# One transformer block on one core: the last 256 tokens as two tiles of 128, and denominators from sums of four key tiles

## The chip, the core and the metric

The kernel runs on one core of a Trainium2 chip. The metric is the device time of one execution in microseconds (us): the median of the runs. Beside the times there is a profile of one execution, taken by the hardware profiler. Engines are called PE (TensorE), ACT (ScalarE), DVE (VectorE), POOL (GpSimd) and SP (SyncE, which issues all DMAs here).

## The reference

x has 2048 tokens of 1024 features, bfloat16. H = 32 heads of 32 features, F = 3584.

```python
def _A_ref(x, wqkv, wo):
    qkv = (x @ wqkv).reshape(B, S, 3, H, Dh)  # then transposed: q, k, v by head
    scores = einsum("bhqd,bhkd->bhqk", q, k) * Dh ** -0.5
    p = softmax(scores, axis=-1)
    o = einsum("bhqk,bhkd->bhqd", p, v)
    return o.transpose(0, 2, 1, 3).reshape(B, S, D) @ wo

def _B_ref(x, w1, b1, w2, b2):
    h = gelu(einsum("bsd,df->bsf", x, w1) + b1, approximate=True)
    return einsum("bsf,fd->bsd", h, w2) + b2

h = x + _A_ref(layernorm(x), A_wqkv, A_wo)
h2 = h + _B_ref(layernorm(h), B_w1, B_b1, B_w2, B_b2)
```

## The kernel before

**Attention.** Four heads make a head group g (0 to 7), and 256 queries a block qb (0 to 7). A job is one (qb, g). It has 8 rounds of two key tiles of 128. `Att.qk` (L769) issues 8 matmuls of a round, four heads side by side in the rows of the array, into two units of two PSUM banks; ACT turns each unit of 1024 columns into P = exp(scale x score) in the ring PT (L779; 9 slots of one round). `Job.pv` (L805) multiplies P by V, four heads side by side in the columns, into one PSUM bank, whose columns 0 to 255 hold O and 256 to 511 the denominators. For these DVE adds the two key tiles of a round into a slot of PS (L820; 3 slots), and `Job.den` (L834) multiplies the sum by a block of ones, 4 matmuls; the last round of a job and the jobs of group 0 of blocks 0 and 1 go to `den` from PT directly, 8 matmuls. `finish` transposes, inverts and multiplies (L850 to L865) and writes OT, which has three slots, taken by u % 3.

**The rest.** Per block u of 256 tokens: `wo(u)` (output projection and residual), `ln2(u)` (LayerNorm, with its statistics on DVE, its powers on POOL, and transposes on PE, L604), `ffn1(u)` (14 blocks of w1, each 16 matmuls of 256 columns), GELU, and `ffn2(u, j)` for the two halves j of the output, each 28 matmuls of 512 columns for each of two token tiles. In blocks 0 to 6 DVE evicts FFN1 with the bias (L943), and GELU is built from five DVE operations and one Tanh on ACT (L962 to L967), for the exp's table holds Tanh too. The last block uses ACT's own GELU (L952) once exps are over (`tail=True`).

**Banks.** Units of scores take banks 0 to 5. Banks 6 and 7 are given out when needed (`Slot`): one bank to a job, for as long as it lasts, the other to the background work. With `tail=True` the banks 0 to 5 are used.

**Order.** No order is written by hand. `Graph.add` records each operation with the buffers that it reads and writes, and `schedule` plays a list scheduler over durations given in the code: `switch` for a change of PE's tiling mode, `c_dve`, `c_dve_ps`, `c_act` and fixed numbers. PE takes, by `pick_pe`, a QK as soon as one is ready, then PV and denominators by how many rounds wait, else background work in the order of the program; with nothing ready, a warming matmul (L1007) at the start. Each engine then executes its list in that order, with semaphore waits between engines. All durations change the order on each engine, but nothing else. Runs of column-tiled matmuls that are long enough are merged into full ones (`merge_tiles`: L537 is such a full matmul, L534 a column-tiled one, L540 one in the tail).

**The lead.** In the first 66 us the 16 rounds of group 0 of blocks 0 and 1 run between LayerNorm, transposes and first projections, on two units of PSUM. Then come the projections of the other groups in between the jobs.

**The end of the program text before:** `wo(6)`, `ffn2(5, ...)`, `ln2(6)`, `ffn1(6)` come after the attention of block 7 in the order of the program; then

```python
    ffn2(6, 0)
    wo(7, True)
    ln2(7, True)
    ffn2(6, 1, True, R1, (None, 5))
    ffn1(7, True)
    ffn2(7, 0, True, R1, (0, 1))
    ffn2(7, 1, True, R2, (2, 3))
```

where R1 are the weight rings that all blocks use, and R2 rings that lie over K and V, which are free by then.

Of the kernel before, what the change touches and what calls it, by code (L numbers as in the profile page):

```python
# [12 lines left out]
P = 128  # L13
# [47 lines left out]
class Graph:  # L61
# [47 lines left out]
    def schedule(self, pick_pe, pool, switch=0.1, dma_rate=280.0, dma_lat=2.1, dma_issue=0.06):  # L109
# [219 lines left out]
def build_kernel(nc, A_x, A_wqkv, A_wo, B_w1, B_b1, B_w2, B_b2, out):  # L329
# [22 lines left out]
    class Area:  # L352
        def __init__(self, start):
            self.cur = start
# [54 lines left out]
    B_OT = [B_OT_[G * i:G * i + G] for i in range(3)]  # L409
    xrb, B_xrb = sb(ot_lo, "xrb", [P, 8, D], BF, 8)  # L410
# [34 lines left out]
    gT7, B_gT7 = sb(Area(pt_lo), "gT7", [P, FC, 256], BF, FC // 2)  # L445
    gs, B_gs = [gT] * 7 + [gT7], [B_gT] * 7 + [B_gT7]
# [22 lines left out]
    att_area = Area(att_lo)  # L469
    w2_area = Area(att_lo)  # L470
    R2 = Rings((att_area, 14), (w2_area, 7), att_area, 2, "b_")
    assert att_area.cur <= att_hi
# [15 lines left out]
    def c_dve_ps(n):  # L488
        return (120 + n) / 960.0 + 0.02

    def c_dve(n, x=1):
        return (62 + n / x) / 960.0 + 0.085

    def c_act(n, ap_bias=False):
        return 0.073 + (0.093 if ap_bias else 0.0) + n / 1200.0

    def pe(fns, occ, reads=(), writes=(), kind="bg", mode="full", prio=0, after=()):
        return gr.add(E.PE, fns, occ, 0.16, reads, writes, prio, kind, mode, after)
# [45 lines left out]
    def act(fn, n, reads=(), writes=(), prio=0, ap_bias=False, kind="", after=()):  # L544
        return gr.add(E.Activation, fn, c_act(n, ap_bias), 0.14, reads, writes, prio, kind, after=after)

    def dve(fn, occ, reads=(), writes=(), prio=0):
        return gr.add(E.DVE, fn, occ, 0.08, reads, writes, prio)
# [25 lines left out]
    def layer_norm(tiles, prio, norm="dve", stats=None):  # L574
# [6 lines left out]
        for k, (x_ap, B_x, o_ap, B_o) in enumerate(tiles):  # L581
            for c in range(2):
                dve(lambda v, c=c, k=k, x_ap=x_ap: v.bn_stats(st_l[:, i + k, 6 * c:6 * c + 6], x_ap[:, 512 * c:512 * c + 512]),
                    0.68, reads=B_x if isinstance(B_x, list) else [B_x], writes=[B_stl[i + k]], prio=(prio or 1) if stats is None else stats)
# [11 lines left out]
        for k, (x_ap, B_x, o_ap, B_o) in enumerate(tiles):  # L596
            eng, cost = (dve, 0.58) if norm == "dve" else (pool, 3.8)
# [4 lines left out]
    def transposes(src_ap, B_src, bank, dst_ap, B_dst, evac, prio):  # L602
# [9 lines left out]
        else:  # L612
            t = dve(lambda v: v.tensor_copy(dst_ap, src()), 0.70, reads=[bb(bank)], writes=[B_dst])
# [133 lines left out]
    class Att:  # L747
# [8 lines left out]
        def qk(self, job, r):  # L756


            qb, g = job
            qs = q_slots[qb, g]  # L760
            us = [self.unit % self.n_units, (self.unit + 1) % self.n_units]
            self.unit += 2
            fns, banks = [], []
            for i in range(2):
                for h in range(4):
                    k0 = (2 * r + i) * P

                    def fn(p, i=i, h=h, k0=k0):
                        return p.matmul(psum[:, 2 * us[h // 2] + h % 2, 256 * i:256 * i + 256],  # L769
                                        KT[32 * h:32 * h + 32, g, k0:k0 + P], QT[32 * h:32 * h + 32, qs, :],  # L770
# [4 lines left out]
            pe(fns, 0.224, reads=[B_KT[8 * g + r], B_QT[qs]], writes=banks, kind="qk", mode="row")  # L775
# [11 lines left out]
    closing = set()  # L787

    class Job:


        def __init__(self, qb, g, bank):
            self.qb, self.g, self.bank = qb, g, bank
            self.B_O, self.B_D = (bank.buf, gr.buf()) if isinstance(bank, Slot) else (B_psO[bank], B_psD[bank])
            self.n = 0
            self.sums = []

        def pv(self, r, s):
            g, bank, first = self.g, self.bank, self.n == 0
            last = self.n == 7  # L800
            self.n += 1
            fns = []
            for i in range(2):
                for h in range(4):
                    fns.append(lambda p, i=i, h=h: p.matmul(  # L805
                        psum[32 * h:32 * h + 32, bi(bank), 0:256], V[:, g, 2 * r + i, 32 * h:32 * h + 32],
                        PT[:, s, h // 2, h % 2, 256 * i:256 * i + 256], start=first and i == 0, stop=last and i == 1,
                        tile_position=(0, 32 * h), skip_group_check=True))
            rd = [B_PT[2 * s], B_PT[2 * s + 1], B_V[NT * g + 2 * r], B_V[NT * g + 2 * r + 1]]
            t = pe(fns, 0.224, reads=rd, writes=[self.B_O, self.B_D] if first else [self.B_O], kind="pv", mode="col")  # L810
# [3 lines left out]
            if r == 7 or (self.g == 0 and self.qb < 2):  # L814
                self.sums.append((s, True))
            else:
# [5 lines left out]
                self.sums.append((n, False))  # L822
# [5 lines left out]
        def den(self, n, direct, last):  # L828
            bank = self.bank
            fns = []  # L830
            for i in range(2 if direct else 1):
                for h in range(4):
                    rhs = PT[:, n, h // 2, h % 2, 256 * i:256 * i + 256] if direct else PS[:, n, h, :]
                    fns.append(lambda p, h=h, rhs=rhs, i=i: p.matmul(  # L834
                        psum[32 * h:32 * h + 32, bi(bank), 256:512], ones32[:, :], rhs,
                        start=False, stop=last, tile_position=(0, 32 * h), skip_group_check=True))
            t = pe(fns, 0.224 if direct else 0.112, reads=[B_PT[2 * n], B_PT[2 * n + 1]] if direct else [B_PS[n]],
# [4 lines left out]
        def finish(self):  # L842
            qb, g, bank = self.qb, self.g, self.bank
            u = qb % 3
# [3 lines left out]
            final = qb == 2 * NCH - 1 and g == G - 1  # L848
            D = OD[:, o, 1, :].rearrange("p (b j) -> p b j", j=32)
            t = dve(lambda v: v.transpose(OD[:, o, 1, :], psum[:, bi(bank), 256:512]), 0.445,  # L850
                    reads=[self.B_O, self.B_D], writes=B_D, prio=-1)
            drop(t, bank)
            if final:
                t = act(lambda a: a.activation(OD[:, o, 0, :], psum[:, bi(bank), 0:256], ACT.Copy), 256,
                        reads=[self.B_O, self.B_D], writes=B_O, prio=-1, after=[t])
            else:
                t = dve(lambda v: v.tensor_copy(OD[:, o, 0, :], psum[:, bi(bank), 0:256]), c_dve_ps(256),  # L857
                        reads=[self.B_O, self.B_D], writes=B_O, prio=-1)
            drop(t, bank)
            dve(lambda v: v.reciprocal(rr[:, o, :], D[:, :, 0]), 0.185, reads=B_D, writes=[B_rr[o]], prio=0)  # L860
            dve(lambda v: v.transpose(D, rr[:, o, :].unsqueeze(2).to_broadcast([P, 8, 32])), c_dve(256),
                reads=[B_rr[o]], writes=B_D, prio=0)
            for k in range(2 if final else 1):
                c = slice(128 * k, 128 * k + 128) if final else slice(0, 256)
                dve(lambda v, c=c: v.tensor_tensor(OT[:, u, g, c], OD[:, o, 0, c], OD[:, o, 1, c], ALU.mult), c_dve(c.stop - c.start),  # L865
                    reads=B_O + B_D, writes=B_OT[u][g][k:k + 1] if final else B_OT[u][g], prio=1)

    pending = []

    def attention_round(job, r, lag=1):  # L870
        s = att.qk((job.qb, job.g), r)
# [14 lines left out]
    def wo(u, tail=False):  # L886
        R = R1
        nb = 0
        R.cnt["w1"] += -R.cnt["w1"] % 4
        ws = [wblock(R, A_wo[:, 256 * k:256 * k + 256]) for k in range(4)]  # L890
        assert ws == [0, 1, 2, 3]
        for t in range(2):
# [3 lines left out]
            for j in range(2):  # L896
                s = ws[2 * j]
# [4 lines left out]
                for k, g in enumerate(order):  # L902
                    mm(bank, OT[:, u % 3, g, t * P:(t + 1) * P], R.w1[:, s:s + 2, g, :], k == 0, k == 7 and not tail,
                       [B_OT[u % 3][g][t], R.B_w1[s], R.B_w1[s + 1]], not tail)
                if tail:
                    mm(bank, ident[:, :], hch[:, hs, c], False, True, [B_ident, B_hch[hs][j]], False)
                    act(lambda a, hs=hs, c=c, bank=bank: a.activation(hch[:, hs, c], psum[:, bank, :], ACT.Copy), 512,
                        reads=[bb(bank)], writes=[B_hch[hs][j]], prio=-1)
                else:
                    drop(dve(lambda v, hs=hs, c=c, bank=bank: v.tensor_tensor(  # L910
                        hch[:, hs, c], psum[:, bi(bank), :], hch[:, hs, c], ALU.add),
                        c_dve_ps(512), reads=[bb(bank), B_hch[hs][j]], writes=[B_hch[hs][j]]), bank)

    def ln2(u, tail=False):
        R = R2 if tail else R1
        for t in range(2):
# [8 lines left out]
    def ffn1(u, tail=False):  # L925
        R = R2 if tail else R1
        for blk in range(FC // 2):
            s = wblock(R, B_w1[:, 256 * blk:256 * blk + 256])
            bank = blk % 6 if tail else slot()
# [5 lines left out]
            if not tail and blk % 2:  # L935
                gelu(u, blk // 2)
# [315 lines left out]
```

## Time and profile before

| | |
|---|---|
| median of 3 runs | 1100.74 us (1100.32 to 1102.1) |
| span of the profiled execution (no time of its own is listed apart) | 1099.2 us, granted PE clock 0.997 |
| busy: PE, DVE, ACT | 1056.5, 757.2, 1019.8 us |
| exps (L779) | 1024, 953.6 us |
| pair sums (L820) | 434, 287.5 us |
| denominator matmuls (L834) | 1736 from PS, 624 from PT |
| end of the last exp | 1031.09 us |
| DMA | 174.43 MB, 159 GB/s over the span |

How to read it: a line of the profile's groups has the line of the code, engine and operation, output and input with their shapes and the count, then the busy time and the mean of one in ns (with the latency, so ones in a row take less), then the engine's idle time just before them and what ended it. In the timeline the columns are start, length, engine, line, operation, count and, in brackets, the idle time before. The busy time of PE counts overlapping matmuls as one stretch, and their ends are modelled.

### The profile page before, as it was taken

To read this page: it belongs to the slowest core of one execution; us is meant where nothing else is said; L and a number is where in the kernel's file an instruction comes from. 1 tells how busy PE (TensorE), PEld (TensorE's weight loads), DVE (VectorE), ACT (ScalarE), POOL (GpSimd) and SP (SyncE) were. 2 spreads that over 40 slices of the span, in tenths; PEclk is the share of its full clock that TensorE was granted. 3 is DMA by queue.
4 is the path that set the end of the run, shared out by engine and by line. 5 is a ranking of instruction groups with operands and counts; after the bars stand their busy time and mean duration, and the time that the engine had idled before them with its cause. 6 is when DMAs were issued, how large, how long until landed. Compare 5 with 4: busy or idle time off the path is not lost.

```text
span 1099.2 us, 42056 instructions
## 1 busy us (share of the span) xinstructions
PE 1056.5 (96%) x19177; PEld 613.8 (56%) x19226; DVE 757.2 (69%) x1444; ACT 1019.8 (93%) x1124; POOL 47.8 (4%) x110
## 2 busy tenths in 40 slices
PE   8899999998899999999999899999999999999998
PEld 6655555553345744664475456546744664565483
DVE  7746666665676886788588768876886787687501
ACT  3879999999999999999999999999999999999650
POOL 3200000000000001001000100010010000000100
PEclk9999999999899999999999999999999999999999
DMA  6820000048345654854576466448654747797370
GB/s 184 227 103 2 29 2 3 2 159 268 115 122 154 189 151 150 260 162 149 185 228 188 150 203 180 143 150 255 181 178 149 216 142 239 243 266 242 98 262 20
DMA packets 265506, 174.43 MB, mean 159 GB/s; under 512 B 26864, under 2 KB 260336, under 8 KB 264560
## 3 DMA queue, kind: packets, MB, share of 16 engines
q1 hardware_dynamic: 265328, 171.74, 51.2%
q8 instruction: 151, 2.47, 0.9%
q14 instruction: 27, 0.22, 0.1%
HBM read 161.23 MB, written 10.49 MB: 156 GB/s over the span
## 4 chain that ended last, share of the span: by engine, by line
ACT 79%; PE 19%; DVE 1%; issue 0%; DMA 0%; POOL 0%; POOLq 0%; DVEq 0%
ACT PT L779 75%; PE ps L540 6%; ACT uu L965 4%; PE ps L537 4%; PE ps L534 3%; PE ps L769 2%; PE ps L805 1%; PE ps L1007 1%; PE ps L834 1%; DMA a_w1r<-in_A_wo_dram 0%; ACT xnT L611 0%; PE ps L604 0%; DVE PS L820 0%; DVE OD L850 0%; DVE OD L857 0%
## 5 line engine op out<-in xcount | busy, mean ns | idle before, releaser
L779 ACT ACTIVATE PT<-ps 128x1024 bf16<-128x1024 f32 x1024 | 953.6, 1189 | 18.2 <-PE ps L769 18.0
L820 DVE TENSOR_TENSOR PS<-PT 128x1024 bf16<-128x1024 bf16 x434 | 287.5, 686 | 124.5 <-ACT PT L779 63.8
L769 PE MATMUL ps<-QT,KT 32*128 32x256 bf16 x4096 | 204.6, 273 | 13.5 <-ACT PT L779 10.2
L805 PE MATMUL ps<-PT,V 128*32 128x256 bf16 x4096 | 179.9, 273 | 1.5 <-ACT PT L779 1.1
L769 PEld LDWEIGHTS ps<-QT,KT 32*128 32x128 bf16 x4096 | 61.0, 92 | 174.1 <-ACT PT L779 165.3
L834 PE MATMUL ps<-PS,ones 128*32 128x256 bf16 x1736 | 121.7, 274 | 2.0 <-DVE PS L820 2.0
L805 PEld LDWEIGHTS ps<-PT,V 128*32 128x32 bf16 x4096 | 103.8, 97 | 30.0 <-issue 8.7
L537 PE MATMUL ps<-a_w2r,gT 128*128 128x512 bf16 x445 | 109.6, 380 | 4.9 <-issue 2.4
L537 PE MATMUL ps<-hnT,a_w1r 128*128 128x256 bf16 x903 | 111.2, 273 | 1.1 <-DVE rr L860 0.5
L534 PE MATMUL ps<-hnT,a_w1r 128*32 128x256 bf16 x2660 | 96.9, 274 | 2.4 <-DVE gT L943 1.2
L537 PEld LDWEIGHTS ps<-hnT,a_w1r 128*128 128x128 bf16 x903 | 82.7, 98 | 25.1 <-issue 14.8
L943 DVE TENSOR_TENSOR gT<-ps,b1f 128x512 bf16<-128x512 f32 x98 | 67.3, 687 | 27.7 <-PE ps L534 18.4
L534 PE MATMUL ps<-a_w2r,gT 128*32 128x512 bf16 x1140 | 81.6, 381 | 2.5 <-DVE OD L857 2.5
L534 PEld LDWEIGHTS ps<-hnT,a_w1r 128*32 128x32 bf16 x2660 | 66.2, 96 | 18.5 <-issue 14.0
L537 PEld LDWEIGHTS ps<-a_w2r,gT 128*128 128x128 bf16 x471 | 40.4, 98 | 55.3 <-issue 15.7
L989 DVE SCALAR_TENSOR_TENSOR hch<-ps,hch 128x512 bf16<-128x512 f32 x32 | 22.0, 689 | 64.0 <-PE ps L540 47.1
L834 PEld LDWEIGHTS ps<-PS,ones 128*32 128x32 bf16 x1736 | 45.9, 96 | 22.8 <-issue 8.7
L965 ACT ACTIVATE uu<-uu 128x1024 bf16<-128x1024 bf16 x49 | 58.0, 1206 | 0.0
L537 PE MATMUL ps<-xnT,Wall 128*128 128x512 bf16 (+1 forms) x213 | 47.7, 360 | 2.3 <-issue 1.1
L588 POOL CAST mvb<-mv 128x2 bf16<-128x2 f32 (+1 forms) x25 | 6.1, 242 | 990.0 <-DVE mv L585 987.2
L706 DVE CAST V<-ps 128x512 bf16<-128x512 f32 x32 | 22.1, 690 | 30.8 <-PE ps L537 15.8
L537 PE MATMUL ps<-Wall,xnT 128*128 128x256 bf16 x327 | 41.0, 273 | 0.0
(85 smaller groups left out, 1009.8 us busy)
## 6 DMA issues: line engine op xcount, KB each, us to landing
a_w2r<-in_B_w_dram SPq DMA_DIRECT2D x105, 512.0 KB, 5.6
a_w1r<-in_B_w_dram SPq DMA_DIRECT2D x98, 512.0 KB, 4.4
a_w1r<-in_A_wo_dram SPq DMA_DIRECT2D x32, 512.0 KB, 4.0
b_w1r<-in_B_w_dram SPq DMA_DIRECT2D x14, 512.0 KB, 5.8
a_w1r<-in_A_wqkv_dram SPq DMA_DIRECT2D x11, 512.0 KB, 4.3
xrb<-in_A_x_dram SPq DMA_DIRECT2D x16, 256.0 KB, 4.2
Wall<-in_A_wqkv_dram SPq DMA_DIRECT2D x16, 256.0 KB, 4.8
hch<-in_A_x_dram SPq DMA_DIRECT2D x16, 256.0 KB, 4.0
```

What stands on the lines that cost most here:

```text
L534: fns.append(lambda p, j=j: p.matmul(psum[32 * j:32 * j + 32, bi(bank), c0:c1], lhsT[:, 32 * j:32 * j + 32], rhs, start=start, stop=stop, ...
L537: t.whole = lambda p: p.matmul(psum[:, bi(bank), c0:c1], lhsT, rhs, start=start, stop=stop, skip_group_check=True)
L540: t = pe(lambda p: p.matmul(psum[:, bi(bank), c0:c1], lhsT, rhs, start=start, stop=stop), occ, reads=reads, writes=[bb(bank)], mode="full" ...
L706: t = dve(lambda v: v.tensor_copy(dst, psum[:, bi(bank), :].rearrange("p (t g c) -> p g t c", t=2, g=2)), c_dve_ps(512), reads=[bb(bank)], ...
L769: return p.matmul(psum[:, 2 * us[h // 2] + h % 2, 256 * i:256 * i + 256], KT[32 * h:32 * h + 32, g, k0:k0 + P], QT[32 * h:32 * h + 32, qs, :],
L779: act(lambda a, u=u, k=k: a.activation(PT[:, s, k, :, :], psum[:, 2 * u:2 * u + 2, :], ACT.Exp, bias=0.0, scale=SCALE), 1024, reads=[B_ps[ ...
L805: fns.append(lambda p, i=i, h=h: p.matmul(psum[32 * h:32 * h + 32, bi(bank), 0:256], V[:, g, 2 * r + i, 32 * h:32 * h + 32], PT[:, s, h // ...
L820: dve(lambda v: v.tensor_tensor(PS[:, n, :, :], pairs[:, :, 0:256], pairs[:, :, 256:512], ALU.add), c_dve(1024, 2), reads=[B_PT[2 * s], B_ ...
L834: fns.append(lambda p, h=h, rhs=rhs, i=i: p.matmul(psum[32 * h:32 * h + 32, bi(bank), 256:512], ones32[:, :], rhs, start=False, stop=last, ...
L943: t = dve(lambda v: v.tensor_tensor(g[:, fc:fc + 2, :], psum[:, bi(bank), :].rearrange("p (f c) -> p f c", f=2), b1f[:, fc:fc + 2].unsquee ...
L965: act(lambda a: a.activation(w, w, ACT.Tanh, bias=0.0, scale=KT2), 1024, reads=[B_uu[i]], writes=[B_uu[i]], prio=-1)
L989: drop(dve(lambda v, hs=hs, bank=bank, half=half: v.scalar_tensor_tensor(hch[:, hs, c], psum[:, bi(bank), :], half, hch[:, hs, c], ALU.mul ...
```

## The change

1. **Sums of four key tiles.** In jobs of 256 queries, rounds 0 and 1, 2 and 3, 4 and 5 are paired (`FOURS`): DVE adds the second round's sum and the first's, and one `den` of 4 matmuls serves both rounds. Round 6 stays alone, round 7 goes from PT.
2. **Half jobs.** Head groups 6 and 7 of block 7 run as jobs of 128 queries with 4 rounds of four key tiles: 16 QK matmuls of 128 columns per round, 16 for PV; first both groups for queries 0 to 127, then both for the others.
3. **The last block by tiles of 128 tokens.** `wo`, `ln2`, FFN1 (`ffn1_half`) and FFN2 (`ffn2_tile`) run for tile 0 with GELU from DVE and Tanh, and for tile 1 with ACT's GELU. FFN1 has 224 matmuls of 128 columns for each tile. Of FFN1's weights 12 blocks of 14 stay in the place of K and V (`W1B`), and both tiles use them; two of the four blocks of Wo are loaded a second time (`WOB`); FFN2's second half has a place of its own in PT (`w2b`).
4. **OT's slots** go by a table (`OS`), and the last block has slot 2.
5. **The planner's durations** are others: latencies and costs of DVE, ACT and PE. In the kernel's instructions they change the order alone.

As built, the exps (1024) and the Tanhs ahead of the last exp (49) keep their count.

```diff
-    def schedule(self, pick_pe, pool, switch=0.1, ...):
+    def schedule(self, pick_pe, pool, switch=0.104, ...):
...
+    OS = [0, 1, 2, 0, 1, 2, 0, 2]
...
-        return (120 + n) / 960.0 + 0.02
+        return (120 + n) / 960.0 - 0.058
...
-        return (62 + n / x) / 960.0 + 0.085
+        return (62 + n / x) / 960.0
...
-        return gr.add(E.DVE, fn, occ, 0.08, reads, writes, prio)
+        return gr.add(E.DVE, fn, occ, 0.135, reads, writes, prio)
...
+    FOURS = (0, 2, 4)
...
                 dve(lambda v: v.tensor_tensor(PS[:, n, :, :], pairs[:, :, 0:256], pairs[:, :, 256:512], ALU.add), c_dve(1024, 2),
                     reads=[B_PT[2 * s], B_PT[2 * s + 1]], writes=[B_PS[n]], prio=-2)
-                self.sums.append((n, False))
+                if nq == 256 and r in FOURS:
+                    self.half = n
+                elif nq == 256 and r - 1 in FOURS:
+                    o = self.half
+                    dve(lambda v: v.tensor_tensor(PS[:, n, :, :], PS[:, n, :, :], PS[:, o, :, :], ALU.add), c_dve(1024, 2),
+                        reads=[B_PS[n], B_PS[o]], writes=[B_PS[n]], prio=-2)
+                    self.sums.append((n, False))
+                else:
+                    self.sums.append((n, False))
...
+    def attention_half(qb, gs, half):
+        for g in gs:
+            if half == 0:
+                load_q(qb, g)
+            job = Job(qb, g, slot(2), P * half, P)
+            for r in range(4):
+                attention_round(job, r)
+        attention_drain()
...
+    def ffn1_half(t, tail):
+        g, B_g = g7[t], B_g7[t]
+        for q in range(FC // 4):
+            bank = q % 6 if tail else slot()
+            for f in range(4):
+                w, B_w = w1_last[2 * q + f // 2]
+                for dc in range(DC):
+                    mm(bank, w[:, dc, (f % 2) * P:(f % 2) * P + P], hnT[:, dc, t * P:t * P + P], dc == 0, dc == DC - 1,
+                       [B_w, B_hnT[t]], not tail, (P * f, P * f + P))
...
-    for u in range(6):
+    for u in range(5):
         wo(u + 1)
...
-        if u < 5:
-            attention(u + 3, range(G))
-    attention_drain()
+        attention(u + 3, range(G) if u < 4 else range(6))
+    attention_half(7, (6, 7), 0)
+    attention_half(7, (6, 7), 1)
+    wo(6)
+    ffn2(5, 0)
+    ln2(6)
+    ffn2(5, 1)
+    ffn1(6)
+    load_w1_last()
     ffn2(6, 0)
-    wo(7, True)
-    ln2(7, True)
-    ffn2(6, 1, True, R1, (None, 5))
-    ffn1(7, True)
-    ffn2(7, 0, True, R1, (0, 1))
-    ffn2(7, 1, True, R2, (2, 3))
+    ffn2(6, 1)
+    wblocks = wo(7, (0,))
+    load_w1_rest()
+    ln2(7, (0,))
+    ffn1_half(0, False)
...
+    wo(7, (1,), True, WOB + wblocks[2:])
+    ln2(7, (1,), True)
+    W20 = ffn2_weights(0)
+    ffn2_tile(7, 0, 0, W20, gT7a, B_gT7a, 0, 0.5, slot(), ())
+    ffn1_half(1, True)
+    W21 = ffn2_weights(1, True)
+    ffn2_tile(7, 1, 0, W21, gT7a, B_gT7a, 0, 0.5, slot(), ())
+    ffn2_tile(7, 0, 1, W20, gT7b, B_gT7b, 0, 1.0, 2, ())
+    ffn2_tile(7, 1, 1, W21, gT7b, B_gT7b, 0, 1.0, 3, ())
```

## The prediction

> **What bounds the kernel now.** I read the page's busy times and slices first, then the waits of ACT from 55 to 1031 us, the groups, and last the timeline of the two ends, where the slices show ACT not full.
>
> ```profile
> span 1099.2 us, 42056 instructions
> ...
> PE 1056.5 (96%) x19177; PEld 613.8 (56%) x19226; DVE 757.2 (69%) x1444; ACT 1019.8 (93%) x1124; POOL 47.8 (4%) x110
> ...
> DVE  7746666665676886788588768876886787687501
> ACT  3879999999999999999999999999999999999650
> ```
>
> ACT is full in all slices but the first three and the last three; DVE is nowhere full; PE looks full, but its matmuls overlap, so its share proves nothing.
>
> ```profile
> ACT PT L779 <- PE ps L769: 9.5, 9, 3.6
> ```
>
> From 55 to 1031 us (976 us) this is the only thing that ACT waits for: 9.5 us in 9 waits, the longest 3.6. All else is ACT's own work, 966.3 us by the windows view: exps and tanhs. Of the 9.5 us, 6.4 lie before 72 us (0.55, 0.58, 1.08, 0.57, 3.65); later there are only 0.76, 0.78, 0.63 and 0.89.
>
> ```profile
> L779 ACT ACTIVATE PT<-ps 128x1024 bf16<-128x1024 f32 x1024 | 953.6, 1189 | 18.2 <-PE ps L769 18.0
> L820 DVE TENSOR_TENSOR PS<-PT 128x1024 bf16<-128x1024 bf16 x434 | 287.5, 686 | 124.5 <-ACT PT L779 63.8
> L834 PE MATMUL ps<-PS,ones 128*32 128x256 bf16 x1736 | 121.7, 274 | 2.0 <-DVE PS L820 2.0
> ```
>
> The 1024 exps are the work that sets the middle; pair sums (L820) and denominator matmuls (L834) lie beside it.
>
> ```profile
> 24.82 1.02 ACT L779 ACTIVATE PT<-ps 128x1024 bf16<-128x1024 f32 x1 [3.82 <-PE ps L769]
> 52.50 1.07 PE L604 MATMUL ps<-ident,xb 128*128 128x128 bf16 x16
> 71.21 49.60 ACT L779 ACTIVATE PT<-ps 128x1024 bf16<-128x1024 f32 x54 [3.65 <-PE ps L769]
> ...
> 1025.48 5.61 ACT L779 ACTIVATE PT<-ps 128x1024 bf16<-128x1024 f32 x6
> 1028.30 2.50 DVE L820 TENSOR_TENSOR PS<-PT 128x1024 bf16<-128x1024 bf16 x4 [3.77 <-PE ps L834]
> 1036.21 1.43 DVE L583 BATCH_NORM_STATS2 st<-hch 128x6 f32<-128x512 bf16 x2 [2.42 <-ACT hch L907]
> 1039.76 0.55 DVE L598 TENSOR_SCALAR b_xb<-hch,mvr,rden 128x1024 bf16<-128x1024 bf16 x1 [1.44 <-POOL rden L594]
> 1041.02 1.02 ACT L611 ACTIVATE hnT<-ps 128x1024 bf16<-128x1024 bf16 x1 [0.96 <-PE ps L604]
> 1047.25 24.62 PE L540 MATMUL ps<-hnT,b_w1r 128*128 128x256 bf16 x224
> 1083.79 12.25 PE L540 MATMUL ps<-b_w2r,gT 128*128 128x512 bf16 x55
> 1096.07 0.69 DVE L989 SCALAR_TENSOR_TENSOR hch<-ps,hch 128x512 bf16<-128x512 f32 x1 [5.35 <-PE ps L540]
> ```
>
> The last exp ends at E = 1031.09. The tail after it, 68.1 us, is PE at its pace: 28 + 4 FFN2 matmuls, Wo, FFN1 (224), FFN2 (112), with under 1 us of gaps; LN2 is hidden behind FFN2 of block 6. So time = lead + ACT's middle + PE's tail.
>
> My sum is made in the profiled span, 1099.2 us; the median, 1100.74, lies 1.5 us above it, and I add that at the end. Runs spread over 1.8 us; 0.2% (2.2 us) is about what a measurement can tell from no change.
>
> **Denominators.** 60 jobs of 256 queries add three sums each. Four matmuls cost PE 0.11 us (weight loads of L834), so 60 x 3 x 0.11 = 19.8 us of PE go. Each sum costs DVE (2.50 - 0.69) / 3 = 0.60 us, so 180 x 0.60 = 108 us come: DVE's 706.6 us of the 976 become 815 (84%). None of that PE time was ACT's wait after 72 us, except in the 3.06 us above. I take 1 us of gain, bounds 0 and 3. In the program as built the background matmuls are hardly further ahead at equal QK rounds (by 0 to 6 us of work, 1 us at the last QK), so the freed PE time is spent as PE idling under ACT. The cover has a price if it goes: a den now waits for two sums, with the next QK queued behind it on PE and the exp behind that. In the heaviest FFN1 stretches DVE has 31 to 32 us of work per 16 rounds by the rows' paces (26 to 27 before), where ACT has 33. I take 0.5 us for such stalls, bounds 0 and 8.
>
> **Half jobs.** Their 16 rounds run QK and PV as 16 matmuls of 128 columns instead of 8 of 256: no row shows these. Between equal column time (no cost) and twice 0.22 us each, that is at most 16 x 0.44 = 7 us of PE, in a stretch where PE has no room: 15 rounds of ACT are 27.5 us, and the old PE work there sums to about 28. QK must end within one exp (0.92) after the release of its unit. I take 1 us of ACT idling, bounds 0 and 4.
>
> **Lead.** The planner's new durations reorder the first 72 us, though no line there is meant to change. As built, ACT alternates exp and xnT copies instead of running two exps and two copies; the second QK comes without the wait for the fourth x tile (0.7 us), and the third before three xnT copies rather than after (up to 2 us). LN chains on DVE and POOL take some back; QT's projection is ahead of the last lead QK by 12 matmuls (0.3 us), which shortens the 3.65. I take 1.5 us of gain, bounds 5 gained and 1 lost.
>
> **Tail.** In the built order nothing of the last block gets ahead of the last exp: after it stand 28 FFN2 matmuls, wo(7) of tile 0 (16), of tile 1 (36 of 256 columns), FFN1 twice with 224 of 128 columns, and four FFN2 tiles. PE's content stays: a 128-column matmul takes (1.07 - 0.22) / 15 = 56.7 ns in the transposes, so 448 x 56.7 = 25.4 us against 224 x 109 = 24.5. One of 512 columns takes 0.216 us ((12.25 - 0.38) / 55; one of the 56 has no record).
>
> [...]
>
> What comes new are gaps. From E, by rows: closing PV and den to 1.2; FFN2 28 x 0.216 to 7.2; wo tile 0 to 10.7; wo tile 1 to 14.6 (36 x 0.109). LN2 of tile 0 starts when tile 0's hch sum ends (11.5); from two statistics to the end of xb took 1036.21 to 1040.31, 4.1 us, so xb is there at 15.4, transposes end at 16.0 and DVE's hnT copy at 16.85. PE idles 14.6 to 16.85 but for 0.45: 1.8 us, where before FFN2 of block 6 lay behind LN2 and now stands in front of wo. Then FFN1 of tile 0 evicts through two banks on DVE, whose queue also holds LN2 of tile 1 and the tanh form of GELU: seven evictions of 0.6, and per 1024 elements 3 x 0.6 + 2 x 0.33. Walking that queue, the sixth eviction ends 1.1 us after PE needs the bank for FFN2, and the last GELUs hold FFN2 0.7 us more: 1.8 us. In sum the matmuls end at E + 68.7 and the last store at E + 71.8 (3.1 for the sum and the store as now): 3.7 more than 68.1; with the gaps hidden or doubled, 0.5 to 6. Who waits behind: FFN1 of tile 1 and all FFN2 are queued behind on PE.
>
> **At nothing.** w1b blocks load into the K and V of finished jobs long ahead. SP queues wob's second block behind four w2b loads that wait for PT slots, free about 3 us before E; 2.5 MB at the 250 GB/s of that stretch take 10 us and land near E + 7, needed at E + 11.6: cover 4 us, a slower landing goes straight to PE. W20 is needed at about E + 28. GELU of tile 1 on ACT: 28 of 128, each some 0.38 us (0.49 for 256 less half its elements), four under 1.8 us of PE. 49 tanhs stay ahead of E.
>
> Sum: -1.5 - 1 + 0.5 + 1 + 3.7 = +2.7; 1100.74 + 2.7 = 1103.4.
>
> **Rivals.** (1) Faster: PE's room pulls ACT's waits shut. If the lead gives 4 us, the middle 3 and the tail costs 2, it ends at 1096. For it: the waits all name PE, and PE loses 19.8 us; against: only 3.06 us of them lie where PE gets the room. It decides from the point where lead and middle give over 5 us. (2) No change: lead and tail cancel, or the built order hides both parts, so that the change does not do what it says: 1100.7. (3) DVE becomes the bound of the six FFN1 stretches; 1 to 1.5 us each is +8, 1109 or 1110. For it: 31 to 32 us against 33; against: DVE gaps of up to 5 us now. (4) 128-column matmuls bound by their weight loads: if the pace were 80 ns, bounded by L604's 57 and by the 98 ns that one weight load is shown with, 448 x 0.024 = +11, so 1114. Against: sixteen in a row at 57. [...]
>
> **How the numbers follow.** Forecast 0.40, its own range 1100 to 1107, 0.10 of it under 1102.9; rival 1 0.28 (0.03 of it above 1098.5); rival 2 0.12; rival 3 0.13; rival 4 0.07. Faster 0.25, same 0.25, slower 0.50. The range goes from 1095 (leaving out a third of rival 1) to 1110 (leaving out rival 4 and the worst of 3).
>
> **What would show it.** Right: the last exp ends within 3 us of 1031, the tail is 71 to 73 us, with about 1.8 us of PE idle behind LN2 and a wait for DVE in FFN1 of tile 0. Den: L857 with a third fewer matmuls, DVE at 79%. Wrong: exps ending before 1026 (rival 1), waits of PE for PS or of ACT for uu over 5 us (rival 3), FFN1 halves over 14 us each (rival 4).

## The result, and the profile after

The changed kernel takes 1109.49 us (median of 4 runs, 1108.03 to 1113.67) against 1101.22 us before on the same chip: ratio 1.0074, 95% interval 1.0052 to 1.0097, so 5.7 to 10.7 us slower. The forecast was 1103.4, in a range of 1095 to 1110. The direction and the range held; the size did not: the forecast is below the interval.

The page of the kernel after: span, busy times, and the slices of DVE and ACT.

```profile
span 1106.6 us, 42516 instructions
...
PE 1045.2 (94%) x19274; PEld 602.2 (54%) x19327; DVE 879.5 (79%) x1661; ACT 1017.4 (92%) x1125; POOL 50.3 (5%) x110
...
DVE  7657777776888996899699879968997988897460
ACT  4879999999999999999999999999999999999431
```

DVE is at the forecast 79%, 122 us more; PE has 11 us less. ACT still sets the middle. In the groups, the sums of a round (432 against 434) and the exps are the same instructions as before, and the added sums (L840) stand by themselves:

```profile
L790 ACT ACTIVATE PT<-ps 128x1024 bf16<-128x1024 f32 x1024 | 957.0, 1197 | 18.3 <-PE ps L779 16.9
L834 DVE TENSOR_TENSOR PS<-PT 128x1024 bf16<-128x1024 bf16 x432 | 294.6, 687 | 96.1 <-ACT PT L790 81.7
L840 DVE TENSOR_TENSOR PS<-PS 128x1024 bf16<-128x1024 bf16 x180 | 123.5, 686 | 3.9
L857 PE MATMUL ps<-PS,ones 128*32 128x256 bf16 (+1 forms) x1056 | 69.9, 269 | 2.2 <-DVE PS L834 1.8
```

ACT's timeline shows where its middle began, each wait of 0.2 us or more in it, and where it ended (start, length, line, count, in brackets the wait ahead):

```profile
68.68 22.13 ACT L790 ACTIVATE PT<-ps 128x1024 bf16<-128x1024 f32 x24 [3.70 <-PE ps L779]
...
254.83 26.12 ACT L790 ACTIVATE PT<-ps 128x1024 bf16<-128x1024 f32 x28 [0.71 <-PE ps L779]
282.56 70.77 ACT L790 ACTIVATE PT<-ps 128x1024 bf16<-128x1024 f32 x77 [1.61 <-PE ps L779]
561.51 9.35 ACT L790 ACTIVATE PT<-ps 128x1024 bf16<-128x1024 f32 x10 [0.40 <-PE ps L779]
653.01 13.87 ACT L790 ACTIVATE PT<-ps 128x1024 bf16<-128x1024 f32 x15 [1.25 <-PE ps L779]
726.04 35.89 ACT L790 ACTIVATE PT<-ps 128x1024 bf16<-128x1024 f32 x39 [0.21 <-PE ps L779]
909.48 42.44 ACT L790 ACTIVATE PT<-ps 128x1024 bf16<-128x1024 f32 x46 [1.22 <-PE ps L819]
953.01 3.77 ACT L790 ACTIVATE PT<-ps 128x1024 bf16<-128x1024 f32 x4 [1.10 <-PE ps L779]
957.43 12.03 ACT L790 ACTIVATE PT<-ps 128x1024 bf16<-128x1024 f32 x13 [0.65 <-PE ps L779]
975.04 12.08 ACT L790 ACTIVATE PT<-ps 128x1024 bf16<-128x1024 f32 x13 [0.94 <-PE ps L779]
...
1010.87 24.11 ACT L790 ACTIVATE PT<-ps 128x1024 bf16<-128x1024 f32 x26
```

By these lines the 7.4 us between the spans are: the lead 2.5 shorter (68.68 against 71.21), the middle 6.4 longer (966.3 from 68.68 to 1034.98, against 959.9), the tail 3.5 longer (71.6 against 68.1). Of the middle's 6.4, 5.0 are waits (8.3 against 3.3), the rest is exps of a slightly longer mean.

Five of the nine waits, 4.3 us, follow a stall of PE's own. The PE timeline ahead of the wait at 653.01:

```profile
650.20 0.49 PE L542 MATMUL ps<-hnT,a_w1r 128*32 128x256 bf16 x10
651.90 0.72 PE L542 MATMUL ps<-hnT,a_w1r 128*32 128x256 bf16 x18 [1.21 <-issue]
652.56 0.40 PE L779 MATMUL ps<-QT,KT 32*128 32x256 bf16 x8
```

"issue" means that PE waited for nothing that the profile shows: no semaphore and no buffer, in the middle of one FFN1 run. Below such a gap is called a stall of PE's own. The QK behind it is late, and ACT with it. From 70 us to the last exp there are 6.7 us of such stalls of over 0.3 us; before, there was one, of 1.0 us at 855.3, with ACT's wait of 0.89 behind it. In the trace's DMA records seven of these eight stalls, and the one before, end 2.3 to 2.6 us after a packet of the instruction queue starts; that queue has 151 packets and 2.47 MB on the page, 16 KB in each.

Of the other four, the 0.71 and the 1.61 lie in stretches in which PE's clock was granted at half (the windows view; PEclk, the third number from the end, is the granted share):

```profile
251.97:255.38 3.41, 3.04 (x36) 1.02 (x40) 2.08 (x3) 2.70 (x4) 0.00 (x0) 0.50 1.14 344
275.86:282.69 6.83, 5.43 (x44) 1.42 (x33) 4.29 (x9) 5.22 (x7) 0.00 (x0) 0.50 0.06 16
```

Everywhere else from 70 us to the last exp the clock is 1.00. Before, there was one such stretch, from 277.61 to 284.44, and the waits of 0.76 and 0.78 lie in it and right behind it. The wait of 0.21 is left open. And the 1.22 us at 909.48 come from DVE, in the timeline of all engines:

```profile
906.00 0.69 DVE L996 TENSOR_TENSOR gT<-uu,gT 128x1024 bf16<-128x1024 bf16 x1
906.75 0.82 PE L545 MATMUL ps<-a_w2r,gT 128*128 128x512 bf16 x3 [0.69 <-DVE gT L996]
907.50 0.40 PE L779 MATMUL ps<-QT,KT 32*128 32x256 bf16 x8
...
908.28 0.69 DVE L1053 SCALAR_TENSOR_TENSOR hch<-ps,hch 128x512 bf16<-128x512 f32 x1 [1.59 <-PE ps L542]
909.02 0.56 PEld L819 LDWEIGHTS ps<-PT,V 128*32 128x32 bf16 x24 [0.43 <-DVE hch L1053]
```

A late GELU product holds FFN2, QK is queued behind it, and the PV that should free a slot of PT waits with its weight loads (PEld) for the sum that frees a bank.

### The profile page after: what moved, and what is told of

The parts are those of the page before. It is cut to its first block, busy times and chain, and to the rows that moved or that the text cites. A ratio compares the mean times of both kernels' runs of the same rounds, so it can differ in the third digit from the quotient of the medians.

```text
span 1106.6 us, 42516 instructions
## 1 busy us (share of the span) xinstructions
PE 1045.2 (94%) x19274; PEld 602.2 (54%) x19327; DVE 879.5 (79%) x1661; ACT 1017.4 (92%) x1125; POOL 50.3 (5%) x110
## 3 DMA queue, kind: packets, MB, share of 16 engines
q8 instruction: 151, 2.47, 0.9%
## 4 chain that ended last, share of the span: by engine, by line
ACT 75%; PE 18%; DVE 5%; issue 1%; POOL 1%; POOLq 0%; DVEq 0%
ACT PT L790 71%; PE ps L545 5%; PE ps L542 4%; ACT uu L994 4%; PE ps L548 2%; PE ps L779 2%; PE ps L819 2%; DVE PS L834 1%; PE ps L1076 1%; PE ps L857 1%; ACT xnT L619 1%; PE ps L612 0%; DVE PS L840 0%; DVE st L591 0%; DVE uu L993 0%
## 5 line engine op out<-in xcount | busy, mean ns | idle before, releaser
L834 DVE TENSOR_TENSOR PS<-PT 128x1024 bf16<-128x1024 bf16 x432 | 294.6, 687 | 96.1 <-ACT PT L790 81.7
L779 PE MATMUL ps<-QT,KT 32*128 32x256 bf16 (+1 forms) x4224 | 204.3, 270 | 11.4 <-ACT PT L790 8.5
L819 PE MATMUL ps<-PT,V 128*32 128x256 bf16 (+1 forms) x4224 | 172.6, 270 | 6.4 <-issue 2.5
L840 DVE TENSOR_TENSOR PS<-PS 128x1024 bf16<-128x1024 bf16 x180 | 123.5, 686 | 3.9
L545 PE MATMUL ps<-hnT,a_w1r 128*128 128x256 bf16 (+1 forms) x912 | 109.6, 271 | 1.2 <-DVE OD L882 0.7
L542 PE MATMUL ps<-a_w2r,gT 128*32 128x512 bf16 x1276 | 92.4, 381 | 1.9 <-DVE OD L882 0.9
L994 ACT ACTIVATE uu<-uu 128x1024 bf16<-128x1024 bf16 (+1 forms) x53 | 63.7, 1216 | 16.2 <-DVE uu L993 16.2
L976 DVE TENSOR_TENSOR gT<-ps,b1f 128x512 bf16<-128x512 f32 x98 | 67.1, 685 | 7.9 <-PE ps L542 5.8
L857 PE MATMUL ps<-PS,ones 128*32 128x256 bf16 (+1 forms) x1056 | 69.9, 269 | 2.2 <-DVE PS L834 1.8
L542 PE MATMUL ps<-xnT,Wall 128*32 128x512 bf16 (+1 forms) x696 | 42.4, 351 | 0.8 <-DVE OD L882 0.6
L542 PEld LDWEIGHTS ps<-a_w2r,gT 128*32 128x32 bf16 x1276 | 28.8, 96 | 25.9 <-issue 13.5
```

The source lines that it names most:

```text
L542: fns.append(lambda p, j=j: p.matmul(psum[32 * j:32 * j + 32, bi(bank), c0:c1], lhsT[:, 32 * j:32 * j + 32], rhs, start=start, stop=stop, ...
L545: t.whole = lambda p: p.matmul(psum[:, bi(bank), c0:c1], lhsT, rhs, start=start, stop=stop, skip_group_check=True)
L779: return p.matmul(psum[:, 2 * us[h // 2] + h % 2, n * i:n * i + n], KT[32 * h:32 * h + 32, g, k0:k0 + P], QT[32 * h:32 * h + 32, qs, q0:q0 ...
L819: fns.append(lambda p, i=i, h=h: p.matmul(psum[32 * h:32 * h + 32, bi(bank), 0:nq], V[:, g, kt * r + i, 32 * h:32 * h + 32], PT[:, s, h // ...
L834: dve(lambda v: v.tensor_tensor(PS[:, n, :, :], pairs[:, :, 0:256], pairs[:, :, 256:512], ALU.add), c_dve(1024, 2), reads=[B_PT[2 * s], B_ ...
L840: dve(lambda v: v.tensor_tensor(PS[:, n, :, :], PS[:, n, :, :], PS[:, o, :, :], ALU.add), c_dve(1024, 2), reads=[B_PS[n], B_PS[o]], writes ...
```

## Experiments

In the table: the ratio to the kernel before with its 95% interval, how far the one profiled run of each lies from the median of its runs, then from that profile the start of the first exp after the lead, the end of the last exp, the tail behind it, ACT's idle time in between, and from 70 us to the last exp the stalls of PE's own of over 0.3 us and the time at half clock (all in us). The profiles lie up to 4 us from their medians, so differences between two profiles of that size say nothing about the kernels.

| kernel | ratio | profile | first | last exp | tail | ACT waits | PE stalls | half clock |
|---|---|---|---|---|---|---|---|---|
| before | 1 | | 71.2 | 1031.1 | 68.1 | 3.3 | 1.0 | 6.8 |
| after | 1.0074 (1.0052 to 1.0097) | -1.0 | 68.7 | 1035.0 | 71.6 | 8.3 | 6.7 | 10.2 |
| durations_alone | 0.9982 (0.9968 to 0.9995) | -4.1 | 68.6 | 1028.2 | 67.1 | 2.9 | 4.8 | 0 |
| sums_alone | 1.0697 (1.0683 to 1.0711) | -2.7 | 71.1 | 1033.4 | 142.5 | 11.5 | 1.2 | 78.5 |
| durations_and_sums | 1.0053 (1.0040 to 1.0066) | -1.1 | 70.5 | 1036.9 | 68.5 | 9.3 | 7.6 | 4.7 |
| all_but_sums | 1.0067 (1.0053 to 1.0080) | -0.8 | 69.6 | 1033.1 | 74.8 | 6.7 | 9.1 | 0 |
| after_merged | 1.0096 (1.0083 to 1.0109) | +2.0 | 69.2 | 1037.3 | 75.5 | 10.2 | 4.6 | 20.5 |
| durations_merged | 0.9959 (0.9946 to 0.9972) | +1.9 | 69.9 | 1031.5 | 67.1 | 4.3 | 5.6 | 0 |
| both_merged | 0.9982 (0.9972 to 0.9992) | +3.2 | 69.3 | 1035.1 | 66.9 | 7.9 | 2.4 | 17.1 |
| wo_ahead_of_ffn2 | 1.0120 (1.0106 to 1.0133) | +1.0 | 70.2 | 1039.1 | 76.4 | 11.2 | 7.8 | 13.7 |
| whole_jobs_new_end | 1.0036 (1.0024 to 1.0048) | -0.7 | 70.1 | 1035.1 | 68.2 | 7.8 | 5.6 | 6.8 |
| whole_jobs_new_end_merged | 1.0010 (0.9998 to 1.0022) | -2.9 | 69.0 | 1030.4 | 68.3 | 3.7 | 0 | 10.2 |
| durations_merged_more | 0.9965 (0.9953 to 0.9977) | +0.9 | 70.1 | 1029.2 | 67.0 | 2.1 | 0.8 | 0 |

**The parts of the change.** Two kernels start from the kernel before, the first with the planner's new durations only, the second with the sums only; the third has both.

```diff
 # durations_alone
-    def schedule(self, pick_pe, pool, switch=0.1, ...):
+    def schedule(self, pick_pe, pool, switch=0.104, ...):
...
 # sums_alone, in Job.pv of before
-                self.sums.append((n, False))
+                if r in FOURS:
+                    self.half = n
+                elif r - 1 in FOURS:
...
+                    self.sums.append((n, False))
```

> The kernel before with nothing but the planner's new durations. In all theories the first exp of the main part starts 2.5 us earlier (68.7 instead of 71.2), for only the order can have moved it. If the sums of four key tiles cost the middle its 6.4 us: ACT's waits after the lead stay near 3 us, the time is about 2.5 under before (1098.5). If the new durations cost it (an order with no margin left): ACT's waits rise to about 8 us and the time is 1103 to 1104. If the half jobs and the new end cost it: 1098.5 too.

> The kernel before with the sums of four key tiles alone, planned with the old durations. Sums at fault: ACT's waits after the lead at 7 to 8 us, lead unchanged at 71.2, tail unchanged at 68: 1105 to 1106. Durations or half jobs at fault: within 1 us of before.

> The kernel before with durations and sums, without half jobs and without the new end. The kernel after less its tail's 3.5 us is 1105 to 1106; expected if sums or durations are at fault. If half jobs and the new end are, 1098.5. The tail is 68 us in each case.

The new durations alone are a gain of 0.5 to 3.5 us; in the profile, the fastest of its twelve runs, 2.6 us of lead and 1.0 us of tail. The sums with the old durations missed all expectations: the order is decided by durations, and with the old ones the planner put the background work of block 6 behind the last exp (42 Tanhs instead of 49 ahead of it), so that the tail is 142.5 us. Its waits in the middle, 11.5 us, are not the sums' own either: 9.9 us of them lie in or within 3 us behind the 78.5 us at half clock. Only together are the two to be read: +5.8 us, and the middle is 966.3 us, as in the changed kernel.

> The kernel after with the sums taken back (each round's sum goes to PE by itself again). Sums at fault: lead 68.7, ACT's waits in the middle about 3 us, tail 71.6: 1102 to 1103. Durations or half jobs at fault: 1108 to 1109, as after.

```diff
-    FOURS = (0, 2, 4)
+    FOURS = ()
```

Without the sums the changed kernel is not faster: the middle is 2.8 us shorter, but 41 FFN2 matmuls stand behind the last exp (28 with the sums), and the tail takes those back. All its waits but one of 0.27 us follow stalls of PE's own, 6.4 us, with no sums and no time at half clock; so such waits are not a price of the sums alone. The three longest stalls, of 1.4 to 1.8 us, lie in the half jobs, the last of them behind the last exp. The PE timeline of all_but_sums there:

```profile
1021.46 0.28 PE L857 MATMUL ps<-PT,ones 128*32 128x128 bf16 x8
1023.18 0.30 PE L857 MATMUL ps<-PT,ones 128*32 128x128 bf16 x8 [1.44 <-issue]
...
1031.46 0.29 PE L819 MATMUL ps<-PT,V 128*32 128x128 bf16 x8
1033.21 0.29 PE L819 MATMUL ps<-PT,V 128*32 128x128 bf16 x8 [1.46 <-issue]
```

A run of 128-column matmuls breaks off halfway, for nothing that the profile shows. That gave the theory: PE is fed by the instruction queue's packets of 16 KB (151 on the page), and a run of small matmuls, each of them two instructions with its weight load, uses them up faster than they come.

**Fewer instructions.** Column-tiled background matmuls come in fours that can be one full matmul. `merge_tiles` does that for runs of 3 us and more; from 0.6 us on, 1,400 to 1,900 matmuls, by kernel, and as many weight loads go, in the same order.

```diff
-            if k == 0 or sum(x.occ for x in run[k:]) >= 3.0:
+            if k == 0 or sum(x.occ for x in run[k:]) >= 0.6:
```

> The kernel after, in which runs of background matmuls in column tiles are made whole from 0.6 us of work on instead of 3.0: 1750 matmuls and weight loads fewer, the order of all else unchanged. If ACT's waits in the middle follow from PE running out of instructions in dense column-tiled runs (stalls named issue, 6.7 us over 0.3 us each after the lead; each ends 2.4 us after a packet of the instruction queue starts): stalls in the middle fall below 2 us, ACT's waits from 8.3 to 4 or 5 us, and the time by 3 to 4 us, to a ratio of 1.004. If DVE, fuller by the sums, is what PE is late for: the waits stay at 8 us and the ratio at 1.007. If the change of tiling mode that each whole run adds costs more than it saves: slower than 1.0075.

> The kernel before with the new durations, and runs made whole from 0.6 us on. Stalls for instructions fall from 4.8 us to under 1.5, ACT's waits from 2.9 to about 1, and the ratio to before from 0.998 to about 0.997, if instructions are what is late; 0.998 if not; over 1 if changes of mode cost.

> Durations and sums without half jobs, runs made whole from 0.6 us on. ACT waited 9.3 us in the middle with 7.6 us of instruction stalls. If these are the cause of two thirds of it: 9.3 falls to 3 or 4, the ratio from 1.0053 to about 1.000. If DVE's load is: no change, 1.005.

With durations and sums, merging brings the ratio from 1.0053 to 0.9982, some 7 us. The waits in the profile of both_merged, 7.9 us, are not the 3 or 4 that were expected, and they have to be split. Those in or within 3 us behind a stretch at half clock rose from 1.0 to 4.7 us; all others fell from 8.3 to 3.0, as the supply theory has it. The stretches at half clock in both_merged:

```profile
252.38:255.79 3.41, 2.63 (x26) 0.76 (x31) 2.07 (x3) 2.58 (x4) 0.00 (x0) 0.50 1.14 362
276.27:283.10 6.83, 5.44 (x44) 1.41 (x33) 4.29 (x9) 5.22 (x7) 0.00 (x0) 0.50 0.03 10
900.91:904.33 3.42, 3.20 (x11) 1.00 (x15) 3.15 (x7) 2.54 (x3) 0.00 (x0) 0.50 0.40 138
1003.31:1006.73 3.42, 3.09 (x21) 0.87 (x14) 3.14 (x7) 2.85 (x3) 0.00 (x0) 0.50 0.63 162
```

With merging in both, the sums still cost 2.5 us (0.9982 against 0.9959). The clock may be that cost: all five runs of durations_merged have a mean granted clock of 1.000, the twelve of both_merged 0.992 to 0.997. It was not tried.

durations_merged gained what was expected in time, but not by fewer stalls: its profile has 5.6 us of them where 4.8 were before and under 1.5 were expected, and 4.3 us of waits instead of about 1. In the changed kernel merging brought nothing, a miss. Of the four stalls of FFN1 one was left, of 0.8 us; two others, of 1.8 and 2.4 us, came in the half jobs, whose QK, PV and denominators can't be merged; and the time at half clock doubled, with 5.6 us of waits in or right behind it (2.3 in the changed kernel).

**LN2 ahead.** This one moves `wo` and `ln2` of tile 0 ahead of the second half of FFN2 of block 6.

```diff
     ffn2(6, 0)
-    ffn2(6, 1)
     wblocks = wo(7, (0,))
-    load_w1_rest()
     ln2(7, (0,))
+    ffn2(6, 1)
+    load_w1_rest()
```

> The kernel after with the text of the end reordered alone: wo and LN2 of tile 0 stand ahead of the second half of FFN2 of block 6, so that LN2 lies behind FFN2 as before the change. If the tail's 3.5 us are the gaps behind LN2 (1.9 us) and DVE's queue in FFN1 of tile 0 (1.3 us): the first vanishes, the second may stay, and the tail is 69 to 70 instead of 71.6; the time falls by 1.5 to 2.5 us. If the tail is longer for its 128-column matmuls: 71.6 stays.

The gap behind LN2 did close, but the kernel became slower still. The last exp ends 4.1 us later, with 2.9 us more of waits. In the tail two stalls came in the closing denominators of the half jobs, 4.8 us. Behind the last exp stand 33 FFN2 matmuls instead of 28, and 6.8 us of the tail are at half clock, so this kernel does not show what the closed gap is worth. Its PE timeline:

```profile
1040.23 0.29 PE L857 MATMUL ps<-PT,ones 128*32 128x128 bf16 x6 [2.50 <-issue]
...
1046.72 0.23 PE L857 MATMUL ps<-PT,ones 128*32 128x128 bf16 x2 [2.31 <-issue]
```

**Without half jobs.** The changed kernel with jobs of 256 queries throughout, and the same with merging from 0.6 us on:

```diff
-        attention(u + 3, range(G) if u < 4 else range(6))
-    attention_half(7, (6, 7), 0)
-    attention_half(7, (6, 7), 1)
+        attention(u + 3, range(G))
+    attention_drain()
```

> The changed kernel with jobs of 256 queries in place of the half jobs; sums, durations and the end by tiles stay. Theory (PE runs out of instructions in dense column-tiled runs, wherever they lie): the middle stays as with durations and sums alone, last exp at 1035 to 1038 us, tail 71 to 72, time 1108 to 1111 (ratio 1.006 to 1.010), no stall over 1 us in the last jobs' PV and denominators. Rival A (the half jobs are themselves what costs, by their 128 columns): last exp 3 us or more earlier than in the changed kernel, ratio 1.004 or less. Rival B (they are a gain, for they let tile 0 go ahead): 4 us slower than the changed kernel.

> The same, with the merging of column-tiled runs from 0.6 us on instead of 3.0 us, which takes some 1,750 matmuls and as many weight loads from PE and leaves their order. Theory: what merging gave with durations and sums (ratio 1.0053 to 0.9982) returns here, for the half jobs with their dense runs are gone: 1101 to 1104, 6 to 8 us below the unmerged one. Rival (merging only shifted the places of the stalls by chance, as it did in the changed kernel, where it gave nothing): within 2.5 us of the unmerged one.

The first is some 4 us faster than the changed kernel by the ratios (1.0036 against 1.0074), and not at the 1108 to 1111 us of the theory. That is the ratio of rival A, but not its mechanism, for the last exp ends where it did (1035.1). The tail is 3.4 us shorter: in the built order 14 FFN2 matmuls of block 6 stand behind the last exp instead of 28. The first rows of its tail on PE:

```profile
1035.75 3.19 PE L545 MATMUL ps<-a_w2r,gT 128*128 128x512 bf16 x14
1038.78 3.62 PE L545 MATMUL ps<-a_w1r,OT 128*128 128x512 bf16 x16
```

With merging, PE's own stalls are gone altogether, the last exp ends 4.8 us earlier, and only three waits are left in the middle: 1.67 and 0.23 us at 282, 1.30 us behind DVE at 907. But this is the fastest of its twelve runs, which reach up to 1106.03 us. The medians differ by 2.5 us, less than the 6 to 8 expected and at the bound of the rival (merging only moves the stalls by chance), so by the times this pair does not decide between the two; the profiles differ by 4.7.

**The supply by itself.** Behind the end of the kernel before, three streams on PE that wait for nothing (their results are not used):

```diff
+    stream(512, 128, True)    # 4 column-tiled matmuls of 128 columns each
+    stream(512, 256, True)    # 4 column-tiled matmuls of 256 columns each
+    stream(1024, 128, False)  # 1 full matmul of 128 columns each
```

> The kernel before, unchanged, and behind its last matmul three streams on PE that wait for nothing and whose results are not used: 2048 column-tiled matmuls of 128 columns, 2048 of 256, and 1024 full ones of 128. Each column-tiled matmul and its weight load are two instructions. Theory: the first stream is not fed fast enough; it shows stalls of PE's own of 0.3 to 2.4 us about once per packet of the instruction queue (some 128 matmuls), and its mean per matmul is well above the pace between the stalls (about 27 ns); the third, at 57 ns for each, shows none or hardly any; the second lies between. Rival (the stalls in the middle come from something else, such as data transfers or the clock): the first stream runs at an even pace, 2048 x 27 ns = 55 us, with no stall over 0.3 us. The time is that of the kernel before and 220 to 300 us.

The PE timeline of that kernel from the end of FFN2 on (L1130 are the column-tiled ones, L1133 the full ones):

```profile
1103.84 1.97 PE L1130 MATMUL ps<-b2t,ident 128*32 128x128 bf16 x128 [1.46 <-issue]
1107.31 1.97 PE L1130 MATMUL ps<-b2t,ident 128*32 128x128 bf16 x128 [1.50 <-issue]
1110.78 1.97 PE L1130 MATMUL ps<-b2t,ident 128*32 128x128 bf16 x128 [1.50 <-issue]
...
1154.62 43.52 PE L1130 MATMUL ps<-b2t,ident 128*32 128x128 bf16 x1536 [1.77 <-issue]
1198.47 15.25 PE L1130 MATMUL ps<-b2t,ident 128*32 128x256 bf16 x533 [0.32 <-issue]
1213.65 57.35 PE L1133 MATMUL ps<-b2t,ident 128*128 128x128 bf16 x1024
```

PE runs 128 matmuls in 1.97 us (15 ns each), stands still for 1.5 to 2.05 us, and runs the next 128, fourteen times over. 128 matmuls and their 128 weight loads are 256 instructions (the trace lists 4096 weight loads of L1130 for its 2048 matmuls of 128 columns and 2048 of 256). The DMA view for 1099 to 1130 us, with nothing else under way but the last store, has the packets:

```profile
q8 instruction: 8, 0.13, 1.7%
```

One packet of 16 KB comes per burst (eight, and eight bursts begin in these 31 us), and each burst begins 2.2 to 2.9 us after a packet's start. The bursts follow each other at 3.47 to 4.02 us. How many packets PE holds, and what sets the time from one to the next, no run here tells. The windows view has the rates:

```profile
1103.84:1154.62 50.78, 27.58 (x1792) 25.55 (x1792) 0.00 (x0) 0.00 (x0) 0.00 (x0) 1.00 0.02 5
1154.62:1198.15 43.53, 43.12 (x1536) 41.48 (x1536) 0.00 (x0) 0.00 (x0) 0.00 (x0) 1.00 0.02 5
```

50.78 us for 1792 matmuls are 28.3 ns each. The column-tiled ones of 256 columns take 43.53 / 1536 = 28.3 ns as well (the first 21 of that row still have 128 columns): they are about as long as the supply took in the first stream, so there is hardly a stall (one of 0.32 us), and no reserve either. The full ones, 57.35 / 1024 = 56 ns, show none. The theory's expectation held for the first and the third; the second stands at the limit rather than between. Two figures missed: the pace inside a burst is 15 ns and not about 27, and the one run took 170.5 us more than the kernel before (1273.02 against 1102.51), not 220 to 300.

**One step further.** The last kernel merges from 0.3 us on (durations new, no other part of the change).

> The kernel before with the planner's new durations and column-tiled background runs merged from 0.3 us on: 868 fewer column-tiled matmuls and 217 more full ones than with the threshold of 0.6 us, in the same order. Theory (supply of instructions): the stalls of PE's own after 70 us, 5.6 us in the profile with 0.6, fall to 3 or less, ACT's waits after the lead from 4.3 to 3 or less, time 1096 to 1098. Rival (below some density the stalls are set by where packets happen to end, not by the count): stalls and time as with 0.6 (1098.4 plus or minus 1.5).

The stalls of PE fell from 5.6 to 0.8 us and ACT's idle time from 4.3 to 2.1, as the supply theory has it. The time, 1097.13 us, lies in the range of the theory and in that of the rival. By the ratios this kernel (0.9965, 0.9953 to 0.9977) and durations_merged (0.9959) are faster than both the kernel before and the changed one; between these two the runs do not tell.

## Why the prediction was right or wrong, point by point

**The shape held.** Time is lead, ACT's middle and PE's tail, each moved as the prediction's signs had it, and DVE at 79% and the 71.6 us of tail are as written; the denominators from PS are 39% fewer (1056 instead of 1736), more than the third it named (its own 60 x 3 x 4 = 720 would be 41%). That the time lies in the range is in part luck: the bound of 8 us that it needed was set for stalls of another kind. The last exp, 3.9 us behind 1031, misses the mark of 3.

**The lead** was to give 1.5 us and gave 2.5 in this profile. The eleven profiles with the new durations have the same order on ACT there, and their first exp starts 0.7 to 2.6 us earlier than in the one profile of before. So the direction and the reason (another order among the first exps and copies) are shown, and the size only to about 1 us.

**Denominators: the step that failed.** The sum had 1 us of gain for the freed matmuls and 0.5 us for stalls of a den that waits for two sums; the middle came out 6.4 us longer. The gain did not come. The middle's loss came near the bound of 8 for stalls, but no wait is that of a den for two sums; the nearest is the 1.22 us at 909, behind DVE's GELU product. Of the 5.0 us of additional waits, 3.4 follow PE running out of instructions (4.3 against 0.9), 1.2 DVE, and 0.8 lie at half clock or right behind it (2.3 against 1.5), with 0.4 less elsewhere. The first and the last of these the prediction did not have. It reckoned PE's work as column time: it never asked how many instructions per microsecond the column-tiled runs need, though before's one stall (1.0 us at 855.3) was in the trace. The streams show such stalls by themselves (1.5 to 2.05 us behind every 128 matmuls), and durations_and_sums against both_merged the size where it binds (1.0053 to 0.9982). But all_but_sums has 6.4 us of such waits without any sums: the reckoning by column time failed for each new order of PE's work, not for the denominators alone. What stays open is why one order runs dense more often than another. The durations alone make 4.8 us of stalls with 2.9 us of waits, in the fastest of their twelve runs; whether the sums take slack that covered such stalls no run shows.

The clock is the other price that was put at nothing. The prediction had the freed PE time "spent as PE idling under ACT". Of the kernels with new durations, the four without sums have no time at half clock in the middle, the seven with sums 4.7 to 20.5 us; the old order had 6.8. In the changed kernel this is the smaller part, 2.3 us of the waits, in both_merged the larger, 4.7 of 7.9.

**Half jobs: nothing at ACT, 3.4 us in the tail.** No wait of ACT lies in their rounds in the changed kernel, so the 1 us set there is nil (in all_but_sums two do, of 0.72 and 1.40 us). Their PV matmuls do run at equal column time in bursts: in the changed kernel 16 of them lie between 1034.89 and 1035.11, 14 ns each, the lower bound of the term. But a half round has 40 matmuls (16 QK, 16 PV, 8 denominators) where a whole one has 20, and at 14 ns they ask for twice what the streams show of supply: so the stalls of 0.50 and 0.96 us at 1019.42 and 1034.37 in the changed kernel and those of 1.4 to 2.5 us in all_but_sums, after_merged and wo_ahead_of_ffn2 are put down to this. The larger bill is one of order: with half jobs the planner has 28 FFN2 matmuls behind the last exp, without them 14. By the two timelines FFN2 begins 0.7 us later after the last exp (1.3 against 0.6) and takes 2.8 us more (5.8 against 3.0), of which the tail shows 3.4.

**Tail: right in size, with a cause unnamed.** The walk met the trace. PE's timeline after the last exp (E = 1034.98):

```profile
1036.30 5.99 PE L545 MATMUL ps<-a_w2r,gT 128*128 128x512 bf16 x27 [0.16 <-issue]
1042.13 3.62 PE L545 MATMUL ps<-a_w1r,OT 128*128 128x512 bf16 x16
...
1050.73 0.62 PE L612 MATMUL ps<-ident,a_xb 128*128 128x128 bf16 x8 [1.06 <-DVE a_xb L606]
1052.14 10.89 PE L545 MATMUL ps<-hnT,w1b 128*128 128x128 bf16 x192 [0.79 <-DVE hnT L621]
1062.87 0.61 PE L612 MATMUL ps<-ident,a_xb 128*128 128x128 bf16 x8
1064.79 1.24 PE L545 MATMUL ps<-a_w2r,gT7a 128*128 128x512 bf16 x5 [1.31 <-DVE gT7a L976]
```

FFN1 of tile 0 begins at E + 17.2 (forecast 16.85; with its own 11.5 + 4.1 = 15.6 for xb, where it wrote 15.4, it would be 17.05); PE waits 1.06 + 0.79 behind LN2 (1.8) and 1.31 for DVE's evictions and GELU (1.8). But the walk took the 28 FFN2 matmuls from the built order as given. whole_jobs_new_end has nearly the same gaps and a tail of 68.2, so in this order it is the half jobs that make the tail long. The end by tiles with its gaps comes out at about the 68.1 of before, which has 28 + 4 FFN2 matmuls there.

**Rivals.** (1) The lead did give, the middle took: not borne out. (2) No change is ruled out by the interval. (3) DVE as the bound fits the time (1109 or 1110) but not the trace: one wait of 1.22 us in the middle is all that is put down to DVE, and merging, which leaves DVE's work as it was, takes out most of the loss in durations_and_sums. (4) FFN1 of tile 0 takes 192 matmuls in 10.89 us, 56.7 ns each, and the stream of full matmuls 56 ns, about half the 109 ns of one of 256 columns before: weight loads add next to nothing, and the half is under 14 us. No run shows the 80 ns of this rival.

## What to carry to other kernels

Count instructions as well as columns: the stream that PE ran at 15 ns for a matmul with its weight load stalled, and came out at 28.3, and a change that cuts matmuls into smaller ones can pay for it there. A stall marked "issue" in the middle of a run of equal matmuls was the sign here, and merging column-tiled matmuls into full ones can help: some 7 us in one kernel here, 2.5 in two, nothing in the changed one. One profile is one execution: look at several before a stall is called a property of the kernel, and look at the granted clock, for here it fell to half in every kernel with the sums, for 4.7 to 78.5 us, and in the one before for 6.8. Where a planner orders the work, its durations and a change of the work belong together, and a part of a change can be tried alone only with durations that fit it.

## What the runs showed of the hardware

- In the stream of column-tiled matmuls of 128 columns the instruction queue brings one packet of 16 KB for each burst of 128 matmuls and their 128 weight loads. A burst takes 1.97 us and the stall behind it 1.5 to 2.05; the mean is one matmul with its weight load per 28.3 ns (1792 in 50.78 us, DMA share 0.02).
- In the kernels themselves such stalls are up to 2.50 us long (wo_ahead_of_ffn2). Of those of over 0.3 us from 70 us to the last exp, seven of the eight in the changed kernel and the only one before end 2.3 to 2.6 us after a packet starts.
- Full matmuls of 128 columns run at 56 ns with their weight loads, 1024 in a row (57.35 us).
- The granted clock falls to 0.50 for 3.41 to 6.83 us at a time in the middle of the kernel before, the changed one and both_merged. Ahead of the two stretches in the changed kernel PE was busy for 1.84 and 2.08 of 3.41 us, ahead of the one before for 1.88. But before, 1.60 us busy of the 3.41 from 608.70 on were not followed by a lower clock. What sets it was not tried.
